# Small tables built ahead of the first loads, and a new order of the work, in a fused retention and token-mixing kernel

## The chip, the cores and the metric

The kernel runs on one core of one Trainium2 chip. A core has five engines with a queue of instructions each, taken in order: TensorE (PE, matrix products), VectorE (DVE), ScalarE (ACT), GpSimd (POOL) and SyncE (SP, which here only issues transfers). They meet through semaphores. The metric is the device time of one execution in microseconds (us).

## The reference, cut to what matters

Inputs are `q`, `k`, `v` of shape (4, 8, 768, 64) in fp32 (batch, heads, tokens, head size) and three weights. The first half is a linear attention with a decay per head:

```python
gamma = 1.0 - 2.0 ** (-5.0 - np.arange(H))
for t in range(S):
    state = gamma * state + einsum('bhd,bhe->bhde', k[:, :, t], v[:, :, t])
    y[:, :, t] = scale * einsum('bhd,bhde->bhe', q[:, :, t], state)
```

The heads of `y` are laid side by side as `x` (4, 768, 512), and the second half mixes tokens:

```python
wq = x @ w_q; wk = x @ w_k                       # 512 -> 64
W_tok = scale * einsum('bsd,btd->bst', wq, wk)   # tokens x tokens
mixed = einsum('bst,btd->bsd', W_tok, x)
out = maximum(mixed, 0) @ w_out
```

## The kernel before, in words

The 768 tokens of a batch are cut into three *pairs* of two chunks of 128 tokens; over four batches that makes pairs 0 to 11. Each pair goes through the same steps. Its `k`, `q` and `v` (512 KB each) are loaded into one of 27 slots of `stage` (`Lk`, `Lq`, `Lv`). They are cast to bf16 (`ck`, `cq`, on ACT, DVE or POOL) and, for `v`, scaled by a table of decay factors (`cv`, always on POOL). PE transposes `k` and `q` (`trk`, `trq`), and the results are copied out of PSUM (`ek`, `eq`). Scores are formed in two halves (`sc`) and masked to be causal while they leave PSUM (`eat`, DVE). The running state is accumulated on PE (`st`) and copied (`es`). The output of the attention sums the state's part (`in`) and the scores' part (`ia`) and is scaled by another table, `fy`, while it leaves PSUM (`ex`, DVE).

The second half of a pair: transpose `x` (`xt`, `exT`), its products with `w_q` and `w_k` (`wqk`, `ew`), a sum over the batch's three pairs (`zm`, `ez`), the mixed tokens (`mx`), their relu (`r`, ACT or DVE), the product with `w_out` in two chunks (`pj`, 512 columns), the copy out (`eo`) and the store (`S`). `W` and `WO` cast the weights. `zm` needs all three pairs of a batch, so the `mx` and `pj` of a batch come after the attention of its last pair.

PSUM has eight banks of 512 fp32 columns; bank 7 holds the state. The digits behind `@` in a step name the banks it uses, so a step also waits until the bank's former content has been copied out.

What sets the order is the string `ORDER` (lines 16 to 61), written out by a planner: one token per step, for instance `ck.3.0:A` (cast half 0 of `k` of pair 3 on ACT), `Lk.4=13` (load into slot 13) or `fill.4@2` (four products of zeros in bank 2, which only keep PE running). The loop at line 826 issues the steps in this order, so that each engine's queue has its share of the string in the string's order. An instruction that waits holds up all that stand behind it on its engine.

`KINDS` (line 63) has a letter for each pair, which says how its tokens lie over the partitions. In kind `2` a partition holds two neighbouring tokens, and both `k` and `v` are cast as they come, each half with one instruction of 128 partitions. Kind `R` has the same load, but `k` and `v` are brought into rows of chunks by two casts of 64 partitions for each half. Kind `M` is `R` for `k`, while `v` is loaded in four pieces of 128 KB (line 177) and cast by one instruction per half, with a table of its own, `fvM`.

The tables: `row` and `tok` (lines 235 to 247) hold each partition's token number; `fv` (line 250) and `fy` (line 255) are exponentials of 48 columns made on ACT at the start, after a product on DVE. The masks of kinds `2` and `R` are made on POOL by the steps `consts.2` and `consts.R` (lines 266 to 284: memset, select, and a copy for the lower 64 partitions). The table `fvM` is made by the step `constv.M` (lines 297 to 307), which stands in `ORDER` between steps of pair 5 and pair 7: two iotas, a copy and a product on POOL and then an exponential on ACT:

```python
        nc.gpsimd.tensor_tensor(out=t, in0=t, in1=ln_n, op=ALU.mult)
        nc.scalar.activation(out=f, in_=t, func=ACT.Exp)
```

`FIRST` (line 64) names the load that is issued ahead of all others in two halves, one from ACT's queue and one from SP's; before it is `q` of pair 0. All other transfers are issued by SP.

Of the kernel before, what the change touches and what calls it, by code (L numbers as in the profile page):

```python
# [16 lines left out]
fill.15@6 Lv.0=1 consts.2 cq.0.1:P cv.0.1:P Lk.0=2 cq.0.0:A Lq.1=3 ck.0.1:A ck.0.0:V Lk.1=4 Lv.1=5  # L17
Lk.2=6 Lq.3=7 consts.R cv.0.0:P Lq.2=8 Lk.3=9 Lv.2=10 cq.1.0:P cq.1.1:P Lv.3=11 ck.1.0:P LW=12
trq.0@0 cv.1.0:P cv.1.1:P Lk.4=13 trk.0@1 Lv.4=14 Lq.4=15 st.0.0 cq.2.1:P Lk.5=16 Lq.5=17 Lv.5=18
LO.1=19 ek.0:A LO.0=20 cq.3.0:P Lk.8=21 Lk.6=22 Lq.6=23 Lv.6=24 Lq.8=25 ck.3.1:P cv.2.0:P eq.0:V  # L20
cv.2.1:P Lk.7=26 es.0.0:V ck.1.1:A fill.1@2 sc.0.1@01 fill.4@2 trq.1@2 Lq.7=0 eat.0.1:V Lv.7=2
cv.3.0:P ck.2.0:A cv.3.1:P Lq.9=1 eq.1:V cv.4.0:P Lv.8=3 Lk.9=4 trk.1@01a Lv.9=5 Lk.10=10 ck.5.1:P
cv.4.1:P st.0.1 sc.0.0@23 ek.1:V es.0.1:V in.0.1@45 ck.2.1:A eat.0.0:V sc.1.0@01 Lq.10=6 eat.1.0:V
cq.2.0:A cq.3.1:A Lq.11=8 fill.3@6 ia.0.0@45 ia.0.1@45 st.1.0 sc.1.1@23 Lk.11=7 es.1.0:V eat.1.1:V
ex.0:V cv.5.0:P in.1.1@01 ia.1.0@01 WO.1:P Lv.10=11 in.1.0@01 ia.1.1@01 trk.2@2 fill.1@6 trq.2@3
ck.3.0:A fill.2@6 trq.3@45a st.1.1 ek.2:V eq.2:V eq.3:A ex.1:V es.1.1:V trk.3@45b sc.2.0@23 cv.5.1:P
eat.2.0:V xt.0@46a ek.3:A exT.0:A xt.1@0 W:A ck.4.0:A ck.4.1:A sc.2.1@15 eat.2.1:V in.2.0@23 st.2.0
fill.1@4 ia.2.0@23 Lv.11=9 es.2.0:V exT.1:V ia.2.1@23 in.2.1@23 st.3.0 sc.3.1@01 ex.2:V eat.3.1:V
sc.3.0@45 es.3.0:A wqk.0@6 xt.2@2 wqk.1@3 exT.2:V eat.3.0:V trk.4@0 ew.0:A cq.4.1:A cq.4.0:A st.3.1
fill.1@1 ia.3.1@26 wqk.2@1 ek.4:A trq.4@45a ck.6.0:P ck.8.1:P es.3.1:V ew.1:V cq.6.0:P in.3.1@26  # L30
ia.3.0@26 ck.5.0:A ck.6.1:P ew.2:V eq.4:V cv.6.0:P zm.0.0@3 zm.0.1@3 cv.6.1:P sc.4.1@45 sc.4.0@01
ez.0:A st.4.0 cq.5.1:A ex.3:V eat.4.1:V eat.4.0:V mx.2@23 es.4.0:A cq.5.0:A trk.5@6 constv.M
ck.7.1:P trq.5@45a xt.3@45b st.4.1 r.2.0:A r.2.1:A in.4.1@23 in.4.0@23 mx.0@01 exT.3:V cq.7.0:P
eq.5:A r.0.0:A ek.5:V ia.4.1@23 ia.4.0@23 wqk.3@4 r.0.1:A es.4.1:A sc.5.1@56 sc.5.0@01 cv.7.0:P
cv.7.1:P cv.8.1:P ex.4:V cv.8.0:P st.5.0 eat.5.0:V WO.0:A xt.4@2 pj.2.1@3 eat.5.1:V eo.2.1:A=12
pj.2.0@0 cv.9.0:P es.5.0:A ia.5.0@13 exT.4:V in.5.0@13 in.5.1@13 mx.1@56 r.1.0:V ia.5.1@13 ex.5:V
ew.3:V eo.2.0:A=12 pj.0.0@0 pj.0.1@2 ck.8.0:A xt.5@13a exT.5:V r.1.1:A eo.0.0:A=13 cq.6.1:A
trk.8@13b trk.6@04a trq.6@04b wqk.4@5 eq.6:A cq.8.0:A ek.8:V ek.6:V wqk.5@6 st.6.0 sc.6.0@04
cq.8.1:A ew.5:A ew.4:V sc.6.1@15 ck.10.1:P zm.1.0@3 ck.7.0:A eo.0.1:V=13 zm.1.1@3 cv.9.1:P eat.6.0:V
eat.6.1:V ez.1:A cq.7.1:A pj.1.1@6 cq.10.0:P cq.10.1:P cq.11.0:P cq.11.1:P trk.7@04a trq.8@04b  # L40
ck.11.0:P ck.11.1:P ek.7:V eo.1.1:A=15 mx.3@23 trq.7@15a pj.1.0@6 r.3.1:A r.3.0:A es.6.0:A eq.8:V
eq.7:V sc.8.1@04 cv.10.1:P cv.10.0:P mx.5@23 st.6.1 eo.1.0:A=15 r.5.1:A cq.9.1:A eat.8.1:V cq.9.0:A
r.5.0:A es.6.1:A ia.6.1@16 ia.6.0@16 in.6.1@16 ex.6:V sc.7.0@05 pj.3.1@4 st.7.0 sc.8.0@16 sc.7.1@23
eat.7.0:V eo.3.1:A=16 es.7.0:A pj.5.1@4 ck.9.0:A ck.9.1:A in.7.0@05 in.7.1@05 st.7.1 eat.7.1:V
ia.7.1@05 eat.8.0:V ia.7.0@05 trq.9@2 pj.3.0@3 ex.7:V xt.6@16a trk.9@16b eo.5.1:A=17 eq.9:A es.7.1:A
mx.4@05 r.4.0:A eo.3.0:V=16 st.8.0 r.4.1:A pj.5.0@2 ia.8.0@34 S.3 es.8.0:A ek.9:V exT.6:V
eo.5.0:A=17 sc.9.0@05 cv.11.0:P in.8.1@34 in.8.0@34 sc.9.1@16 st.9.0 S.5 es.9.0:A ck.10.0:A
eat.9.0:V ia.8.1@34 cv.11.1:P wqk.6@2 xt.7@0 pj.4.0@5 ew.6:A ex.8:V eat.9.1:V trk.10@2 st.9.1
trq.10@34a xt.8@34b in.9.1@16 eo.4.0:V=14 exT.7:A ek.10:A eq.10:V ia.9.0@16 ia.9.1@16 ex.9:V
pj.4.1@2 sc.10.1@05 exT.8:A eo.4.1:A=14 trq.11@34b sc.10.0@16 trk.11@34a wqk.8@2 eat.10.1:V ek.11:V  # L50
# [24 lines left out]
def kernel(  # L75
# [17 lines left out]

    nc = tc.nc
# [6 lines left out]
    U = 2  # L101
# [25 lines left out]
    def bank16(b):  # L127
        return banks[:, b].bitcast(BF16)
# [31 lines left out]
    def load(name, p, slot, part=None, eng=None):  # L160
# [7 lines left out]
        if KINDS[p] == "N" and name != "q":  # L168
# [60 lines left out]
    def iota(t, pattern, base, step, dtype=FP32):  # L229
# [5 lines left out]
    row = const_pool.tile([128, 3], mybir.dt.int32, name="row")  # L235
    tok = const_pool.tile([128, 1], FP32, name="tok")
# [5 lines left out]
    nc.vector.tensor_scalar(  # L242
        out=row[:, 1:2], in0=row[:, 0:1], scalar1=1, scalar2=U * (TG - 1), op0=ALU.logical_shift_left,
        op1=ALU.bitwise_and,
    )
    nc.vector.tensor_single_scalar(row[:, 2:3], row[:, 0:1], 6, op=ALU.logical_shift_right)
    nc.vector.tensor_tensor(out=tok, in0=row[:, 1:2], in1=row[:, 2:3], op=ALU.add)
# [635 lines left out]
```

## Time and profile before

| | |
|---|---|
| median of 3 runs | 153.59 us (152.68, 157.84, 153.59) |
| the profiled execution | 154.91 us, span of its instructions 153.2 us |
| mean granted TensorE clock in it | 0.833 |
| moved by DMA | 26.73 MB, of it 20.19 MB read from HBM |
| DMA busy share in 40 slices | near full until about 70 us, then low until the stores |

How to read the profile: times count from the span's start. "Busy" is the time in which an engine executed something. In a list of waits, `A <- B` means that an engine stood idle ahead of an instruction of line A until B released it. In a list in order of time each row has the start, the length, the engine, the line, the tiles (out<-in), the shape, the count, and in brackets the idle time ahead of it and what ended that. A busy PE is not a PE at its peak, since matmuls are pipelined. Rows of neighbouring instructions of one line are merged, under the first one's shape.

### The profile page before, as it was taken

The page shows a single profiled execution, that of the slowest core. Times are in us where ns is not written, and L with a number is a line of the kernel's source. Part 1 is how long each engine was busy: PE and PEld are TensorE (multiplying, and loading weights), DVE is VectorE, ACT ScalarE, POOL GpSimd, SP SyncE. Part 2 cuts the span into 40 slices and gives each one's busy share as a digit, 9 for nine tenths or more (in the row PEclk, how much of TensorE's full clock was granted, in tenths as well). Part 3 has the DMA queues.
Part 4 walks back from the last instruction along what each step waited for, and adds up shares of the span by engine and source line. Part 5 has one row for each costly group of instructions (what it writes and reads, how often), then busy time and mean ns, then how long its engine had stood idle before and what let it go on. Part 6 is the DMA issues. An engine that isn't in the chain of part 4 may idle for free.

```text
span 153.2 us, 3907 instructions
## 1 busy us (share of the span) xinstructions
PE 102.7 (67%) x1667; PEld 70.4 (46%) x1684; DVE 72.9 (48%) x117; ACT 65.4 (43%) x116; POOL 60.6 (40%) x89
## 2 busy tenths in 40 slices
PE   6958875599720997865365674569573766495990
PEld 2345554588520763743342443257452655263440
DVE  4045994567760376483533413143725733433460
ACT  4154256619404737537510705244244160435541
POOL 7599779879396699999100000000000000000000
PEclk9986999659985589999857655556999699999999
DMA  3999999999999999984000000342000000076394
GB/s 96 346 347 347 343 279 287 336 315 288 273 282 300 322 296 283 287 187 95 4 0 0 4 0 0 137 166 112 0 4 0 0 0 4 0 295 255 147 351 191
DMA packets 47169, 26.73 MB, mean 174 GB/s; under 512 B 8240, under 2 KB 44080, under 8 KB 47152
## 3 DMA queue, kind: packets, MB, share of 16 engines
q1 hardware_dynamic: 46624, 26.22, 56.1%
q10 hardware_dynamic: 528, 0.26, 0.6%
q8 instruction: 13, 0.21, 0.5%
q14 instruction: 4, 0.03, 0.1%
HBM read 20.19 MB, written 6.29 MB: 173 GB/s over the span
## 4 chain that ended last, share of the span: by engine, by line
PE 37%; SPq 21%; DVE 17%; ACT 9%; DMA 5%; issue 5%; POOL 4%; DVEq 0%; ACTq 0%; POOLq 0%
SPq L182 17%; PE banks L805 12%; DVE at L555 6%; DMA stage<-in_k_dram 5%; DVE x L685 5%; ACT relu L798 5%; PE banks L537 3%; SPq L199 3%; PE banks L664 3%; PE banks L727 2%; PE banks L738 2%; ACT qT L145 2%; PE banks L764 2%; DVE kT L146 2%; PE banks L694 2%
## 5 line engine op out<-in xcount | busy, mean ns | idle before, releaser
L805 PE MATMUL banks<-wout_sb,relu 128*128 128x512 bf16 x84 | 23.9, 406 | 9.5 <-DVE x L685 3.5
L555 DVE TENSOR_TENSOR at<-banks,maskR 128x1024 bf16<-128x1024 f32 x18 | 21.6, 1220 | 18.0 <-PE banks L537 7.6
L382 POOL TENSOR_TENSOR vs<-stage,fv 64x512 bf16<-64x512 f32 x24 | 25.0, 1043 | 2.9 <-DMA stage<-in_v_dram 1.5
L685 DVE TENSOR_TENSOR x<-banks,fy 128x1024 bf16<-128x1024 f32 x12 | 14.7, 1221 | 17.8 <-PE banks L664 7.7
L145 ACT COPY stage<-banks 128x512 f32<-128x512 f32 x15 | 8.7, 588 | 23.5 <-DVE at L555 6.9
L805 PEld LDWEIGHTS <-relu 128*128 128x128 bf16 x96 | 9.1, 103 | 18.4 <-issue 10.5
L145 ACT CAST ks<-stage 64x512 bf16<-64x512 f32 (+1 forms) x23 | 14.1, 616 | 6.6 <-DMA stage<-in_k_dram 6.3
L798 ACT ACTIVATE relu<-banks 128x512 bf16<-128x512 f32 x19 | 10.8, 597 | 11.8 <-PE banks L805 6.2
L146 POOL CAST ks<-stage 64x512 bf16<-64x512 f32 (+1 forms) x18 | 11.0, 609 | 5.7 <-DMA stage<-in_k_dram 5.0
L537 PE MATMUL banks<-qT,kT 64*128 64x128 bf16 x144 | 9.0, 263 | 5.7 <-DVE at L555 2.3
L328 PE MATMUL banks<-warm 128*128 128x512 bf16 x23 | 9.6, 575 | 1.8 <-DVE warm L218 1.3
L146 DVE COPY stage<-banks 128x512 f32<-128x512 f32 x9 | 6.1, 688 | 9.5 <-ACT relu L798 7.0
L537 PEld LDWEIGHTS <-kT 64*128 64x128 bf16 x144 | 6.0, 115 | 7.9 <-issue 6.6
L610 PE MATMUL banks<-s,qT 64*128 64x64 bf16 x128 | 4.2, 206 | 8.0 <-ACT relu L798 7.7
L664 PE MATMUL banks<-vs,at 128*128 128x64 bf16 x144 | 7.8, 209 | 2.6 <-DVE at L555 2.5
L727 PE MATMUL banks<-xT,wqk_w 128*128 128x256 bf16 x48 | 8.6, 309 | 1.4 <-DVE at L555 1.4
L145 ACT CAST qs<-stage 128x512 bf16<-128x512 f32 x13 | 7.7, 619 | 3.8 <-DMA stage<-in_q_dram 3.8
L555 DVE TENSOR_TENSOR at<-banks,mask 128x1024 bf16<-128x1024 f32 x6 | 7.2, 1222 | 3.6 <-ACT wqk_w L145 1.6
L571 PE MATMUL banks<-vs,ks 128*64 128x64 bf16 (+1 forms) x200 | 8.0, 217 | 1.3 <-POOL vs L363 0.9
L738 PE MATMUL banks<-wqk_w,xT 128*128 128x64 bf16 x96 | 8.7, 268 | 0.0
L664 PEld LDWEIGHTS <-at 128*128 128x128 bf16 x144 | 6.5, 108 | 4.5 <-issue 3.5
L146 DVE COPY kT<-banks 128x1024 bf16<-128x1024 bf16 x8 | 5.4, 685 | 5.9 <-PE banks L664 3.1
(89 smaller groups left out, 165.5 us busy)
## 6 DMA issues: line engine op xcount, KB each, us to landing
stage<-in_k_dram SPq DMA_DIRECT2D x12, 512.0 KB, 6.4
stage<-in_q_dram SPq DMA_DIRECT2D x11, 512.0 KB, 7.0
stage<-in_v_dram SPq DMA_DIRECT2D x9, 512.0 KB, 6.9
out_dram<-stage SPq DMA_DIRECT2D x9, 512.0 KB, 2.9
stage<-in_v_dram SPq DMA_DIRECT2D x12, 128.0 KB, 3.8
out_dram<-stage SPq DMA_DIRECT2D x6, 256.0 KB, 2.0
stage<-in_moe_w_out_dram SPq DMA_DIRECT2D x4, 256.0 KB, 4.5
stage<-in_q_dram ACTq DMA_DIRECT2D x1, 256.0 KB, 4.1
```

The source lines that it names most:

```text
L145: return nc.scalar.copy(out=out, in_=in_)
L146: return ENGINES[e].tensor_copy(out=out, in_=in_)
L182: eng.dma_start(out=st.rearrange("g (h f) -> g h f", h=H)[:, hs], in_=src.rearrange("h (g j) d -> g h (j d)", j=2)[:, hs],)
L382: eng.tensor_tensor(out=st["vs"][rows(j), c].rearrange("p hp x d -> p (hp x) d"), in0=src[rows(c), :, j], in1=fv[rows(c), cp, :, j].to_bro ...
L537: nc.tensor.matmul(out=at[:, x, hi, c], lhsT=kT[rows(x), hp, c], rhs=qT[rows(x), c, hp], start=(hi == 0 and c == 0), stop=(hi == 1 and c = ...
L555: ENGINES[e].tensor_tensor(out=st["at", half].rearrange("p x hi j t -> p x (hi j t)").rearrange("p x (n f) -> p x n f", n=n), in0=st["at_p ...
L664: nc.tensor.matmul(out=y[:, x, c, hp, :], lhsT=at[:, x, hi, c, :], rhs=vr[:, c, hp, x, :], start=first(p, x), stop=False, skip_group_check ...
L685: ENGINES[e].tensor_tensor(out=dst, in0=src, in1=f.to_broadcast([128, 2, H, D]), op=ALU.mult)
L727: nc.tensor.matmul(out=ps[:, 128:384], lhsT=wqk_sb[:, a, 0 : 2 * DH], rhs=st["xT"][:, a].rearrange("p c t -> p (c t)"), start=(a == 0), st ...
L738: nc.tensor.matmul(out=wk[:, c], lhsT=st["xT"][:, a, c, :], rhs=wqk_sb[:, a, 2 * DH :], start=False, stop=(a == NDM - 1), skip_group_check ...
L798: nc.scalar.activation(out=st["relu", c], in_=src, func=ACT.Relu)
L805: nc.tensor.matmul(out=bank32(b[0]), lhsT=st["relu", c][:, a // 2, a % 2, :], rhs=wout_sb[:, a, :], start=(a == 0), stop=(a == NDM - 1),)
```

## The change

It has three parts.

- **Tables and masks.** The tables of all kinds are made at the start: `decay` forms the product on DVE and the exponential on ACT, for `fy` and, behind it, for the table of kind `M` (`fvm`). The masks are made on DVE by comparing a row of token numbers, `tf` (an iota on POOL), with each partition's token number. The steps `consts` and `constv` are gone from `ORDER`, and no mask is made on POOL. The identity for the transposes stays on POOL and comes before the masks.
- **Kinds.** `KINDS` goes from `2R2RRR2RRMMM` to `2RR2R2RRRMRM`: pairs 0, 3 and 5 are of kind `2` (before 0, 2 and 6), and 9 and 11 of kind `M` (before 9, 10 and 11).
- **Order.** `FIRST` is `k` of pair 1. The whole `ORDER` is new, with the engine of each cast and copy: one `cv` is now on DVE, more casts of `k` are on ACT and fewer on POOL, both casts of `w_out` are on POOL, and the loads of `w_out` come behind those of pair 6.

`U` becomes a constant of the module with the value that it had; branches for `U == 8` are added and not taken. `trq` is rewritten with the same transposes.

The core of the diff; of `ORDER` only the stretches that the prediction speaks of:

```diff
-ez.0:A st.4.0 cq.5.1:A ex.3:V eat.4.1:V eat.4.0:V mx.2@23 es.4.0:A cq.5.0:A trk.5@6 constv.M
-ck.7.1:P trq.5@45a xt.3@45b st.4.1 r.2.0:A r.2.1:A in.4.1@23 in.4.0@23 mx.0@01 exT.3:V cq.7.0:P
...
+fill.15@6 Lq.0=1 cq.0.0:V ck.1.1:A cq.0.1:A Lk.0=2 Lv.0=3 trq.0@0 Lq.1=4 Lv.1=5 ck.1.0:P Lk.2=6
+Lq.3=7 Lq.2=8 Lv.2=9 eq.0:V ck.0.0:V cv.0.0:V fill.2@1 trk.1@12a Lk.3=10 LW=11 Lv.3=12 cv.0.1:P
+Lq.4=13 Lk.4=14 ck.0.1:A Lv.4=15 Lq.5=16 Lk.5=17 cv.1.0:P cq.3.1:P cv.1.1:P Lk.6=18 fill.6@3 trk.0@0
+cv.2.0:P Lv.5=19 Lv.6=20 Lq.6=21 LO.1=22 ck.3.1:P LO.0=23 Lk.7=24 Lk.8=25 cv.2.1:P ek.0:V Lq.7=26
...
+ck.5.1:A ck.7.0:P cv.6.1:P in.4.0@36 zm.0.1@0 xt.3@2 ez.0:A trk.5@5 st.4.1 eat.4.1:V in.4.1@36
+trq.5@1 cv.7.0:P cq.8.0:P ck.6.0:A cv.7.1:P ek.5:A ck.6.1:A ia.4.0@36 exT.3:V es.4.1:V eq.5:V
...
+pj.1.0@0 eat.6.0:V eo.1.1:V=11 es.6.0:V pj.2.0@4 ck.8.1:A ck.8.0:A eo.1.0:V=11 sc.6.1@26 mx.0@05
+cq.7.0:A eo.2.0:V=13 xt.5@13a trk.7@13b cq.7.1:A eat.6.1:V r.0.1:A ek.7:V r.0.0:V pj.2.1@4 st.6.1
...
-KINDS = "2R2RRR2RRMMM"
-FIRST = ('q', 0, 0)
+KINDS = "2RR2R2RRRMRM"
+FIRST = ('k', 1, 0)
...
+    def decay(name, tok, ln):
+        t = const_pool.tile([128, NP * 2, H], FP32, name="t" + name)
+        f = const_pool.tile([128, NP * 2, H], FP32, name=name)
+        nc.vector.scalar_tensor_tensor(out=t, in0=ty, scalar=tok, in1=ln, op0=ALU.add, op1=ALU.mult)
+        nc.scalar.activation(out=f, in_=t, func=ACT.Exp)
+        return f
+
+    fy = decay("fy", tok_q, ln_h)
+    fvs = {}
+    if "M" in KINDS:
+        fvs["M"] = decay("fvm", tok_r, ln_n)
...
+    def mask(name, toks):
+        t = const_pool.tile([128, len(toks), C], BF16, name=name)
+        for j, tok in enumerate(toks):
+            nc.vector.tensor_scalar(out=t[:, j], in0=tf, scalar1=tok, scalar2=None, op0=ALU.is_ge)
+        return t
...
-    def mask(name, nj, step, base2):
...
-            nc.gpsimd.memset(a, 1.0)
-            nc.gpsimd.affine_select(
...
-    def consts_v(kind):
...
-        nc.gpsimd.tensor_tensor(out=t, in0=t, in1=ln_n, op=ALU.mult)
-        nc.scalar.activation(out=f, in_=t, func=ACT.Exp)
-        fvs[kind] = f
```

More of the change, by code (lines that the diff above doesn't have):

```diff
@@ L22 @@
[L22 to L26, printed above, removed]
@@ L232, in iota @@
         )
-    row = const_pool.tile([128, 3], mybir.dt.int32, name="row")
-    tok = const_pool.tile([128, 1], FP32, name="tok")
+    row = const_pool.tile([128, 6], mybir.dt.int32, name="row")
     iota(row[:, 0:1], [[0, 1]], 0, 1)
@@ L390, in cq @@
         st = pairs[p]
+        if U == 8:
+            if "qs" not in st:
+                st["qs"] = new("qs", [128, U, 2, D])
+            copy(e, st["qs"][:, :, x], st["q_st"].rearrange("p (x u d) -> p x u d", x=2, u=U)[:, x])
+            return
         if "qs" not in st:
```

197 lines of the change are left out of this document (97 added, 100 removed).

## The prediction

> **What bounds the kernel now.** I read the page first, then the waits, then three engines' instructions in order of time around the longest wait, then busy time by stretch.
>
> ```profile
> PE 102.7 (67%) x1667; PEld 70.4 (46%) x1684; DVE 72.9 (48%) x117; ACT 65.4 (43%) x116; POOL 60.6 (40%) x89
> ...
> PE 37%; SPq 21%; DVE 17%; ACT 9%; DMA 5%; issue 5%; POOL 4%; DVEq 0%; ACTq 0%; POOLq 0%
> ```
>
> No engine is full, and the chain that ended last changes hands between PE, DVE and ACT. So the time lies in who waits for whom. The waits, longest first, have one pair that stands out:
>
> ```profile
> PE banks L610 <- ACT relu L798: 7.7, 2, 6.3
> ...
> ACT fvM L306 <- POOL tvM L305: 7.0, 1, 7.0
> ```
>
> ScalarE (ACT) stood still once for 7.0 us ahead of the exponential that `constv.M` issues, and TensorE (PE) once for 6.3 us. They are one event, as the three engines show in order of time (start, length, instruction):
>
> ```profile
> 40.60 0.62 ACT L145 CAST qs<-stage 128x512 bf16<-128x512 f32 x1
> 48.22 0.24 ACT L306 ACTIVATE fvM<-tvM 128x48 f32<-128x48 f32 x1 [7.00 <-POOL tvM L305]
> 48.37 1.06 ACT L798 ACTIVATE relu<-banks 128x512 bf16<-128x512 f32 x2
> ```
> ```profile
> 34.23 2.14 POOL L382 TENSOR_TENSOR vs<-stage,fv 64x512 bf16<-64x512 f32 x2 [0.74 <-DMA stage<-in_v_dram]
> ...
> 42.03 1.96 POOL L146 CAST ks<-stage 128x512 bf16<-128x512 f32 x3 [2.33 <-DMA stage<-in_k_dram]
> ...
> 47.91 0.28 POOL L305 TENSOR_TENSOR tvM<-tvM,ln_n 128x48 f32<-128x48 f32 x1
> 49.29 1.28 POOL L146 CAST ks<-stage 64x512 bf16<-64x512 f32 x2 [1.10 <-DMA stage<-in_k_dram]
> ```
> ```profile
> 36.87 0.60 PE L727 MATMUL banks<-xT,wqk_w 128*128 128x256 bf16 x4
> 37.31 0.61 PE L738 MATMUL banks<-wqk_w,xT 128*128 128x64 bf16 x8
> ...
> 39.42 0.62 PE L537 MATMUL banks<-qT,kT 64*128 64x128 bf16 x16
> ...
> 41.22 0.40 PE L783 MATMUL banks<-m,z 64*128 64x256 bf16 x4 [0.93 <-ACT qs L145]
> ...
> 42.92 0.32 PE L571 MATMUL banks<-vs,ks 128*64 128x64 bf16 x8
> 49.49 0.61 PE L610 MATMUL banks<-s,qT 64*128 64x64 bf16 x16 [6.26 <-ACT relu L798]
> ...
> 51.30 1.04 PE L727 MATMUL banks<-xT,wqk_w 128*128 128x256 bf16 x4
> 52.14 1.06 PE L738 MATMUL banks<-wqk_w,xT 128*128 128x64 bf16 x8
> 53.13 1.04 PE L537 MATMUL banks<-qT,kT 64*128 64x128 bf16 x16
> ```
>
> To be read from the bottom up: PE at 49.49 (`in.4`) waits for a bank that ACT's relu of pair 2 must empty. That relu's input was there at 41.62 (41.22 + 0.40), but on ACT it stands behind the exponential, which needs the table that GpSimd (POOL) multiplies at 47.91. POOL was late because `ck.6`, ahead of it, waited for its load until 42.03. A table of 48 columns thus tied PE to a load of another pair. Busy time by stretch:
>
> ```profile
> core 0: us, PE busy (x) PEld busy (x) DVE busy (x) ACT busy (x) POOL busy (x), PEclk, DMA share, GB/s
> 0.00:11.00 11.00, 8.17 (x48) 3.62 (x48) 3.17 (x36) 3.91 (x7) 7.85 (x24) 0.98 0.87 259
> 11.00:41.20 30.20, 23.82 (x524) 18.73 (x529) 21.34 (x28) 16.65 (x28) 24.77 (x28) 0.84 1.07 314
> 41.20:49.50 8.30, 1.84 (x54) 1.48 (x54) 3.42 (x4) 1.30 (x5) 6.04 (x12) 0.71 0.94 275
> ...
> 70.00:128.40 58.40, 36.31 (x602) 26.48 (x608) 23.50 (x24) 22.64 (x42) 3.49 (x4) 0.74 0.09 31
> 128.40:153.20 24.80, 15.43 (x131) 8.02 (x132) 9.64 (x13) 9.42 (x17) 0.00 (x0) 1.00 0.50 191
> ```
> ```profile
> 49.50:54.50 5.00, 5.00 (x73) 3.87 (x73) 1.46 (x2) 3.13 (x5) 3.75 (x6) 0.50 1.09 324
> ```
>
> POOL leads until 41.2 (24.77 of 30.2 us), and is all but done by 70. From 70 on only PE, DVE (VectorE) and ACT work, each with gaps, for 83.2 us of 153.2.
>
> **The change, part by part.** I sum against the profiled execution: 154.91 us, span 153.2, so 1.7 lie around the span. The median of the three times is 153.59, which is 1.3 lower; at the end I take that off.
>
> *1. The table `fvM`.* Its product and exponential move to the start, behind `fy`. The ACT wait of 7.0 goes; what the path has of it is PE's 6.26. What is late next? Without the wait the two relus (1.06) start at about 41.65 and end at 42.7, before PE has finished at 43.24 (42.92 + 0.32); `in.4.1` can then follow at once. So 6.3 goes in full: **-6.3**. Were something else late there, it would be zero.
>
> *2. The slow matmuls behind the gap.* The granted clock was 0.50 from 49.5 to 54.5, and groups that took 0.60, 0.61 and 0.62 before the gap took 1.04, 1.06 and 1.04 after it. With no gap these three give back 0.44 + 0.45 + 0.42 = 1.3. The most would be 5.00 us of PE at 0.50 made at 1.00, thus 2.5; the least is nothing, if the new order has a gap of its own. DVE and ACT have work between the groups, so I take the three: **-1.3**. [...]
>
> *3. The masks.* POOL loses two memsets, two selects and a copy for each of two masks. The first set ended before its first cast; the second lies between two `cv` steps:
>
> ```profile
> 7.82 0.29 POOL L273 TENSOR_SCALAR_AFFINE_SELECT maskR<-maskR 128x128 bf16<-128x128 bf16 x1
> 8.06 0.20 POOL L272 MEMSET maskR_b<- 128x128 bf16 x1
> 8.33 0.35 POOL L273 TENSOR_SCALAR_AFFINE_SELECT maskR_b<-maskR_b 128x128 bf16<-128x128 bf16 x1
> 8.75 0.29 POOL L283 COPY maskR<-maskR_b 64x128 bf16<-64x128 bf16 x1
> 9.12 1.05 POOL L363 TENSOR_TENSOR vs<-stage,fv 128x512 bf16<-128x512 f32 x1
> ```
> ```profile
> 8.00 0.55 DVE L146 CAST ks<-stage 128x512 bf16<-128x512 f32 x1 [4.67 <-DMA stage<-in_k_dram]
> ```
>
> That frees up to 1.5 us of POOL at 7.6 to 9.1. In the new order `cv.0.1` has no such work ahead, but v of pair 0 is now the fourth half-megabyte and not the second; one covers the other, so 0 (bounds -1.5 and 0). DVE gets three compares of 128 columns and a few one-column operations. The trace has no such compare; below the cast of 512 columns (0.55), above nothing: I take 0.2 each, 1 us with the small ones, all inside the 4.67 us in which DVE waited for its first load. If that cover were gone it would cost that 1 us. ACT's third small exponential (0.24 by the row at 48.22) stands ahead of `ck.1.1` and lies in its wait for the first load.
>
> *4. `cv.0.0` on DVE* (0.6 us by the cast's row, at most the 1.05 of POOL's) beside POOL's `cv.0.1`: both wait for v of pair 0, and behind `cv.0.0` on DVE stands `ek.0`, for which PE's first scores wait. It ends before POOL's, which the first state step needs too: 0. [...] The nearest row, the select at 8.33 beside DVE's cast, took 0.35 where its twin took 0.29; no row here has the pair itself. [...]
>
> *5. Casts change hands.* By the two orders ACT has 26 half-tile k casts instead of 20, one more whole one, three more q casts, two more of xT and three more of kT; it loses two of qT, a weight cast, a z, a relu and one output copy, and has one more of s.
>
> ```profile
> L382 POOL TENSOR_TENSOR vs<-stage,fv 64x512 bf16<-64x512 f32 x24 | 25.0, 1043 | 2.9 <-DMA stage<-in_v_dram 1.5
> ...
> L145 ACT CAST ks<-stage 64x512 bf16<-64x512 f32 x20 | 12.3, 616 | 2.3 <-DMA stage<-in_k_dram 2.0
> ```
>
> At 0.6 a cast and 1.0 a transposed tile ACT gains about 7 us; POOL loses as much, DVE gains 1. Up to the step `st.4.1` (42.92 above), ACT had about 20 us of such work; in the new order about 26 (10 half-tile and 4 whole k casts 8.6, 9 of q 5.6, 8 tiles of kT, qT and xT 8.1, weights 1.1, 5 of s and one z 2.3). It has to fit between 11 and 41.2 us, where ACT was busy 16.65 of 30.2: nothing is lost if the six go into the gaps, 6.0 if none does. DVE lived with 21.34 in the same stretch; with six more ACT has 22.7. That is the nearest row, so I stay near the lower end: **+1.5**.
>
> *6. Loads.* Bytes are the same, and so each half-megabyte lands when its place in the queue did. k of pair 6 moves from place 22.5 to 18.5, where v of pair 5 came at 34.23: 7.8 us earlier than 42.03. k of pair 7 goes from 26.5 (49.29) to 24.5, k of 8 to 25.5, q of 7 to 26.5: about 45.6, 47.5, 49.3. With k of pair 1 in front, q of pair 0 comes one place later, some 1.5 us; but k of pair 0, which the first scores need, stays third (8.00 in the rows of part 3). SP issues the later loads with fewer waits, since the slots are free long before. One pair fewer has its v in four pieces, for which POOL pays two casts of 1.043 more (in POOL's count above). Nothing on the path: 0.
>
> *7. The new order after 56 us.* The same matmuls but for nine more warm-up fills, early, in front of waits for loads; the order from the last `ia.11` on has twelve `pj` steps in both, seven of them after the last `mx`, so the last 24.8 us stay. Between, no PE wait is longer than this one:
>
> ```profile
> PE banks L537 <- DVE at L555: 2.3, 1, 2.3
> ```
>
> so one such more or less: 0, bounds -2.3 and +2.3.
>
> Sum: 154.91 - 6.3 - 1.3 + 1.5 = 148.8, and with the 1.3 to the median **147.5 us**.
>
> **The rivals.**
> *A. ACT bounds the front.* All six us of part 5 land on the path: 4.5 more, 152.0. For it: ACT takes its work in order, and its casts wait for loads. Against it: 13.5 us of ACT's stretch are idle.
> *B. Slower: PE at half rate.* If ACT, filled with casts, hands out banks in bursts, PE gets gaps like the one at 43 again, and the clock stays at 0.50 where it was 0.74 (70 to 128.4). PE has 37% of the chain: 21.6 of these 58.4 us become 32.0, 10.4 more: 157.9. It decides from a mean below about 0.60 on. For it: 0.74 shows how near it is. Against it: the longest wait there is 2.3.
> *C. More gain.* The six us vanish into gaps, the slow matmuls give back 2.5 and one wait of 2.3 goes: 147.5 - 1.5 - 1.2 - 2.3 = 142.5. Beyond that the loads stop it: `cq.7.0`, ahead of a relu on ACT, can't run before 49.3.
> *D. The table isn't what held PE.* If another of pair 4's inputs came at 49 as well, parts 1 and 2 are nothing: 153.59 + 1.5 = 155.1. Its conditions (bank, state, qT) were all met by 43 in the rows above, which speaks against it.
>
> **How the numbers follow.** The forecast, 145 to 150.5: 0.50. C: 0.13. A: 0.15, D: 0.06, both within 2%, which is about what a measurement of this kernel can tell from no change (150.5 to 156.7). B: 0.16. So faster 0.63, same 0.21, slower 0.16. Eight in ten: from 142 (C) to 155.5 (past A and D); B and a bit more stay out.
>
> **What would show it.** After: the exponentials all before 4 us; no ACT wait for POOL of several us; PE without a gap over 3 us between 35 and 55, clock 0.7 or more there (parts 1, 2); `st.4.1` at 41 to 45 (part 5); ACT near 72 us, POOL near 53; the end 24 to 26 us after the last `ia.11`. Wrong would be: a new long wait of PE for ACT behind a k or q cast, or a clock below 0.6 in the long middle.

## The result, and the profile after

The changed kernel takes **165.67 us** (median of four runs, 165.25 to 170.26); the kernel before took 154.25 us beside it. The ratio is **1.077 [1.067, 1.087]**: slower, where the forecast was 147.5 and faster. Some executions of each of these kernels run a few per cent longer at a lower granted clock: the ratios, here and further down, leave them out (a cell is empty where there is no ratio), the medians don't, and the profiled execution, 170.26 us with a span of 168.5 at a clock of 0.737 (0.75 to 0.77 in the others), is one of them, so what follows goes by where time stands in it and not by differences of a few us.

Busy time of the changed kernel by engine, from the page:

```profile
PE 117.9 (70%) x1694; PEld 78.1 (46%) x1709; DVE 74.5 (44%) x124; ACT 73.0 (43%) x126; POOL 53.3 (32%) x67
```

ACT and POOL are where the forecast had them (72 and 53). TensorE is busy 15 us longer with nearly the same instructions: its mean granted clock was 0.74, for 0.83 before. By stretch of time (busy us of each engine, granted clock, DMA share, GB/s):

```profile
core 0: us, PE busy (x) PEld busy (x) DVE busy (x) ACT busy (x) POOL busy (x), PEclk, DMA share, GB/s
0.00:11.00 11.00, 9.56 (x61) 4.17 (x64) 5.46 (x44) 4.46 (x9) 4.21 (x13) 1.00 0.88 263
11.00:41.20 30.20, 18.78 (x368) 13.79 (x370) 14.44 (x15) 16.59 (x27) 21.64 (x23) 0.69 1.08 318
41.20:49.50 8.30, 6.83 (x127) 5.70 (x121) 2.11 (x3) 1.08 (x2) 6.00 (x8) 0.50 1.12 330
49.50:56.50 7.00, 4.46 (x44) 3.24 (x44) 2.86 (x4) 3.25 (x6) 5.70 (x7) 0.50 1.05 293
...
143.00:168.50 25.50, 17.72 (x128) 8.53 (x128) 8.55 (x12) 7.98 (x14) 0.00 (x0) 0.89 0.32 124
```

The stretch 11 to 41.2 is the one to compare with the same row of before. There PE made 524 matmuls and VectorE (DVE) 28 instructions; here it is 368 and 15. PE, DVE and POOL work less, and ACT no more than before (16.59 for 16.65), where the forecast put 22.7 into the same time. Nothing became the bound; the engines wait more. How far this runs, by the scaling of pair 3 (`ex.3`) of before, and then the same step and the step `st.4.1` of after:

```profile
39.94 1.23 DVE L685 TENSOR_TENSOR x<-banks,fy 128x1024 bf16<-128x1024 f32 x1 [0.82 <-ACT z L145]
```
```profile
53.66 1.23 DVE L704 TENSOR_TENSOR x<-banks,fy 128x1024 bf16<-128x1024 f32 x1 [2.49 <-PE banks L556]
...
60.02 0.42 PE L590 MATMUL banks<-vs,ks 128*64 128x64 bf16 x8
```

`ex.3` is 13.7 us late, and `st.4.1`, at 42.92 before and forecast for 41 to 45, is 17.1 late. The whole loss (11.4 us by the medians) is there before 60 us.

Who waits for whom? The groups of the mask product and of the scaling in the changed kernel, with the idle time ahead of them and its three largest releasers:

```profile
L574 DVE TENSOR_TENSOR at<-banks,maskR 128x1024 bf16<-128x1024 f32 x18 | 21.8, 1220 | 23.7 <-PE banks L824 5.6 <-ACT stage L145 5.0 <-PE banks L683 4.0
L704 DVE TENSOR_TENSOR x<-banks,fy 128x1024 bf16<-128x1024 f32 x12 | 14.6, 1220 | 16.1 <-PE banks L824 5.8 <-PE banks L683 4.2 <-PE banks L556 4.1
```

This is the odd part. The scaling (L704) reads the attention's output, which L629 and L683 make. Line 824 is the product with `w_out`, line 556 the scores of another pair: neither makes anything that the scaling reads. One case in order of time, the scaling of pair 1 (`ex.1`, banks 1 and 5), first PE, then DVE:

```profile
24.77 0.27 PE L629 MATMUL banks<-s,qT 64*128 64x64 bf16 x7 [1.18 <-DVE x L704]
26.13 0.61 PE L517 MATMUL banks<-identity,qs 64*128 64x64 bf16 x16 [1.09 <-ACT kT L145]
...
29.51 0.61 PE L556 MATMUL banks<-qT,kT 64*128 64x128 bf16 x8 [0.36 <-issue]
```
```profile
27.82 0.69 DVE L146 COPY qT<-banks 128x1024 bf16<-128x1024 bf16 x1 [3.11 <-ACT qT L145]
30.16 1.22 DVE L704 TENSOR_TENSOR x<-banks,fy 128x1024 bf16<-128x1024 f32 x1 [1.65 <-PE banks L556]
```

Its input was complete at 25.04 (24.77 + 0.27). It started at 30.16, when the scores `sc.2.1@03` had ended (29.51 + 0.61 = 30.12). Those go to banks 0 and 3, and bank 3 lies between 1 and 5. The copy ahead of it on DVE, `eq.3` out of bank 2, had waited 3.11 us for ACT's `eq.2` out of banks 0 and 3, and bank 2 lies between those. From this came the theory of the **ranges**: an instruction that takes two banks in one strided access waits for what other engines do in any bank from the lower to the upper, not in its own two alone. The digits in `ORDER` allow a count. Of the 102 steps of before that name two banks, 56 name neighbours, and among the first 60 steps with banks 32 of 37 do. In the new order it is 31 of 104, and at the start 4 of 35 (`@03`, `@15` and `@46` are the usual ones). The rivals against it: casts that fill ACT (rival A of the prediction), and the clock as a cause of its own (rival B).

The trace and `ORDER` together also allow a count of the waits themselves. In the kernel before, 22 waits of ACT or DVE of over 0.15 us ahead of a copy or product out of PSUM (49.4 us in all) ended with such an instruction on the other engine. In 16 of them (38.4 us) the two share no bank, but their ranges meet; in five (8.6 us) they share one; one (2.4 us) fits neither. In the changed kernel it is 15 of 20 (42.7 of 50.5 us), two and three, and the last three (6.7 us) aren't explained by ranges.

### The profile page after: what moved, and what is told of

Same layout as the page of the kernel before. It is cut to its first block, busy times and chain, and to the rows that moved or that the text cites. A ratio compares the mean times of both kernels' runs of the same rounds, so it can differ in the third digit from the quotient of the medians.

```text
span 168.5 us, 3951 instructions
## 1 busy us (share of the span) xinstructions
PE 117.9 (70%) x1694; PEld 78.1 (46%) x1709; DVE 74.5 (44%) x124; ACT 73.0 (43%) x126; POOL 53.3 (32%) x67
## 5 line engine op out<-in xcount | busy, mean ns | idle before, releaser
L824 PE MATMUL banks<-wout_sb,relu 128*128 128x512 bf16 x85 | 28.8, 467 | 9.6 <-ACT relu L817 3.8
L574 DVE TENSOR_TENSOR at<-banks,maskR 128x1024 bf16<-128x1024 f32 x18 | 21.8, 1220 | 23.7 <-PE banks L824 5.6
L399 POOL TENSOR_TENSOR vs<-stage,fv 64x512 bf16<-64x512 f32 x28 | 29.2, 1043 | 8.3 <-DMA stage<-in_v_dram 6.9
L704 DVE TENSOR_TENSOR x<-banks,fy 128x1024 bf16<-128x1024 f32 x12 | 14.6, 1220 | 16.1 <-PE banks L824 5.8
L145 ACT CAST ks<-stage 64x512 bf16<-64x512 f32 (+1 forms) x30 | 18.5, 617 | 3.0 <-DMA stage<-in_k_dram 2.7
L145 ACT COPY xT<-banks 128x1024 bf16<-128x1024 bf16 x7 | 7.1, 1015 | 17.1 <-PE banks L802 7.7
L145 ACT COPY kT<-banks 128x1024 bf16<-128x1024 bf16 x7 | 7.0, 1012 | 14.3 <-DVE at L574 5.7
L345 PE MATMUL banks<-warm 128*128 128x512 bf16 x33 | 11.5, 486 | 2.4 <-DVE warm L224 1.2
L746 PE MATMUL banks<-xT,wqk_w 128*128 128x256 bf16 x48 | 11.0, 375 | 2.6 <-DVE xT L146 1.8
L146 DVE COPY qT<-banks 128x1024 bf16<-128x1024 bf16 x9 | 6.1, 688 | 12.1 <-PE banks L629 4.4
L757 PE MATMUL banks<-wqk_w,xT 128*128 128x64 bf16 x96 | 10.6, 304 | 0.0
L145 ACT CAST s<-banks 128x256 bf16<-128x256 f32 x15 | 5.6, 374 | 10.0 <-PE banks L590 10.0
L757 PEld LDWEIGHTS <-xT 128*128 128x128 bf16 x96 | 9.4, 154 | 1.1
L683 PE MATMUL banks<-vs,at 128*128 128x64 bf16 x144 | 7.5, 212 | 3.3 <-ACT relu L817 3.3
```

Source lines behind the costliest of these rows:

```text
L145: return nc.scalar.copy(out=out, in_=in_)
L146: return ENGINES[e].tensor_copy(out=out, in_=in_)
L345: nc.tensor.matmul(out=bank32(b), lhsT=warm[:, 0:128], rhs=warm, start=True, stop=True)
L399: eng.tensor_tensor(out=st["vs"][rows(j), c].rearrange("p hp x d -> p (hp x) d"), in0=src[rows(c), :, j], in1=fv[rows(c), cp, :, j].to_bro ...
L574: ENGINES[e].tensor_tensor(out=st["at", half].rearrange("p x hi j t -> p x (hi j t)").rearrange("p x (n f) -> p x n f", n=n), in0=st["at_p ...
L683: nc.tensor.matmul(out=y[:, x, c, hp, :], lhsT=at[:, x, hi, c, :], rhs=vr[:, c, hp, x, :], start=first(p, x), stop=False, skip_group_check ...
```

## The experiments

All times are medians. The kernel before ran beside each group on the same chip and took 154.3 to 156.2 there. "Tables alone", "renamed", "spread" and "split" are told below, each where its runs come.

| kernel | us | against before |
|---|---|---|
| changed kernel | 165.67 | 1.077 [1.067, 1.087] |
| tables alone | 148.06 | |
| changed, banks renamed | 130.23 | |
| before, banks renamed | 133.16 | 0.856 [0.843, 0.870] |
| before, banks spread | 184.45 | |
| tables alone, banks renamed | 122.61 | 0.799 [0.795, 0.804] |
| changed, renamed up to `st.4.1` | 144.38 | 0.939 [0.929, 0.948] |
| changed, renamed from `st.4.1` on | 147.82 | 0.956 [0.941, 0.971] |
| changed, six casts to POOL | 181.46 | 1.174 [1.155, 1.193] |
| changed, split | 106.36 | 0.686 [0.673, 0.700] |
| changed, renamed and split | 104.64 | 0.679 [0.671, 0.687] |
| before, spread and split | 114.23 | 0.741 [0.732, 0.750] |
| before, split | 113.94 | 0.742 [0.734, 0.751] |
| tables alone, split | 101.55 | 0.654 [0.643, 0.666] |
| tables alone, renamed and split | **101.06** | 0.654 [0.640, 0.668] |
| changed, split, `cv.0.0` on POOL | 103.63 | 0.674 [0.663, 0.685] |
| changed, only DVE's products split | 127.41 | 0.823 [0.808, 0.838] |

### The tables alone

The changed kernel with `KINDS`, `FIRST` and the string `ORDER` of before; only the steps `consts.2`, `consts.R` and `constv.M` are taken out of the string.

```diff
-KINDS = "2RR2R2RRRMRM"
-FIRST = ('k', 1, 0)
+KINDS = "2R2RRR2RRMMM"
+FIRST = ('q', 0, 0)
```

> The new tables and masks with the order, kinds and first load of before. If the wait of ACT for the table fvM held PE for 6.3 us, as the prediction's parts 1 and 2 have it, this runs 6.3 to 7.6 us faster than before: 146.5 to 148. If something else of pair 4 or 5 came as late (rival D), it stays within 2 us of before. If making the tables on VectorE at the start costs, it is slower.

148.06 (146.13 to 150.35) beside 154.75: 6.7 faster, and 6.9 by the two quickest executions (146.13 and 146.42) against the three quickest of before (152.21 to 153.71). So parts 1 to 3 of the prediction, 7.6 together, hold. Everything else in the change (parts 4 to 7, forecast at +1.5) makes the 148.06 into 165.67, 17.6 us longer; what loses lies in the new order.

### Renaming the banks

The digits of `ORDER` go through a list before they are used; nothing else changes, neither the order of the steps nor the engines, nor which steps share a bank. (The two digits of a step are sorted after it, so the halves of a pair can swap banks.) In the changed kernel 62 of the 104 pairs then are neighbours (31 before), in the kernel before 71 of 102, and in the spread one 4 of 102.

```diff
+BANK = (1, 2, 5, 0, 6, 3, 4)
...
-            b = ["ab".index(i) if i in "ab" else int(i) for i in b]
+            b = sorted(BANK[int(i)] for i in b if i not in "ab") + ["ab".index(i) for i in b if i in "ab"]
```

For the kernel before the list is `(2, 1, 6, 5, 4, 3, 0)`, and spread `(3, 1, 2, 5, 0, 6, 4)`.

> The changed kernel, with nothing but the seven PSUM banks of the order renamed among themselves (0 to 6 become 1,2,5,0,6,3,4), so that the pairs of banks used together lie side by side more often. Theory (spans): a step that touches two banks b0 and b1 also waits for steps on the banks between them, and the new order has such pairs far apart in its first third; then this is at least 6 us faster than the changed kernel, 160 or less. Rival (casts): ACT, filled with casts, bounds the front; the names of banks change nothing, 165 to 166. Rival (clock): the granted clock is low because PE draws more; again 165 to 166.

> Before, with nothing but its banks renamed (0 to 6 become 2,1,6,5,4,3,0), which brings pairs closer in its last two thirds. Spans: faster by 2 to 6 us, 148 to 152, with the 7 us wait for the table still there. Casts or clock: within 1 us of before.

> Before, with its banks renamed so that pairs lie far apart (0 to 6 become 3,1,2,5,0,6,4). Spans: slower by 8 us or more, 162 or more, with VectorE and ScalarE waiting in the first third as they do in the changed kernel. Casts or clock: within 1 us of before, since no engine gets other work.

The order of before takes 133.2, 154.8 and 184.5 us with 71, 56 and 4 neighbouring pairs; the new order takes 130.2 and 165.7 with 62 and 31. The names alone move each kernel by more than any part of the change was forecast to. With good names the changed kernel is no slower than the one before, though ACT does the same work as in the changed kernel with its own names, by the page of the renamed one:

```profile
PE 94.9 (74%) x1694; PEld 62.6 (49%) x1709; DVE 73.5 (58%) x124; ACT 72.6 (57%) x126; POOL 53.2 (42%) x67
```

So rival A doesn't explain the slowdown. What the fuller ACT costs beside it isn't shown here: the tables alone, with renamed banks, are still faster than this kernel (next run). PE's 94.9 us, for 117.9 with the same matmuls, show the clock: its mean in the profiled executions is 0.93 here and 0.74 in the changed kernel, 0.90 and 0.73 in the kernel before with good and with spread names. Only the names differ within each of the two, so the clock follows the waits and isn't a cause of its own.

### The tables with renamed banks

The two edits above together: the tables alone, with the list `(2, 1, 6, 5, 4, 3, 0)`.

```diff
+BANK = (2, 1, 6, 5, 4, 3, 0)
```

> The order of before, with the tables of after (as in the run with the tables alone, 148.1) and with the banks of before renamed 2, 1, 6, 5, 4, 3, 0 (as in the run that took before from 154.8 to 133.2). If the table of pair 9 to 11 and the ranges of banks are two independent losses, the 6.7 of the tables comes off the 133.2: about 126.5. If the wait for the table was partly a wait for banks, 130 to 133.

122.61 (122.49 to 122.99), 10.6 below the renamed kernel before (8.9 by the two ratios). Independent losses would have given 6.7; that the late table costs more once other waits are gone is shown further down. The renamed changed kernel, with the new order besides, took 130.23 (its quickest execution 125.53). So with good names too the new order gains nothing; it costs 7.6 by the medians and 3.0 by the quickest executions.

### Where the ranges cost

The list is used only ahead of `st.4.1`, as in the diff, or (with `False`) only from there on. At the border some banks are written under their new name before they have been read under the old one, so these two compute something else from there; the instructions are the same.

```diff
+LAST = ORDER.index("st.4.1")
...
+            m = BANK if (n < LAST) == True else range(7)
```

> The changed kernel with the banks renamed 1, 2, 5, 0, 6, 3, 4 only in the steps ahead of st.4.1 (which came at 60.0 in after, at 42.9 in before). Ranges of banks, acting where they stand: the first 60 us lose about 17 us, the rest keeps its length, so 147 to 150. If a delay of the front is all there is, and the rest followed from it: 130, as with all steps renamed. If the names of the banks worked in another way than by the ranges in the steps that use them: 165.

> The changed kernel with the banks renamed only in the steps from st.4.1 on. Ranges of banks, acting where they stand: st.4.1 stays at 60 and the rest gives what the other run doesn't, so 146 to 150 (the two gains add up to the 35 of the whole renaming). If a delay of the front is all there is: 165.

144.38 and 147.82: 21.3 and 17.9 below the changed kernel, 39.2 together, where the whole renaming gave 35.4 by the medians and 39.7 by the quickest execution of each. So the ranges act where they stand, in both halves. The front, which lost 17, gives back somewhat more than it lost.

### Casts from ACT to POOL

```diff
-sc.0.0@45 fill.1@6 sc.1.1@12 sc.1.0@03 es.0.1:V eat.0.0:V eat.1.1:V eat.1.0:V ck.2.1:A fill.2@6
-ia.0.1@46 in.0.1@46 cv.5.0:P cv.5.1:P in.1.0@15 st.1.0 ia.0.0@46 cq.3.0:A ck.2.0:A Lk.10=7 Lk.11=6
-trq.3@2 Lq.10=12 fill.2@0 trk.2@03a ia.1.1@15 ia.1.0@15 cq.2.1:A es.1.0:A cq.2.0:A ex.0:V in.1.1@15
+sc.0.0@45 fill.1@6 sc.1.1@12 sc.1.0@03 es.0.1:V eat.0.0:V eat.1.1:V eat.1.0:V ck.2.1:P fill.2@6
+ia.0.1@46 in.0.1@46 cv.5.0:P cv.5.1:P in.1.0@15 st.1.0 ia.0.0@46 cq.3.0:P ck.2.0:P Lk.10=7 Lk.11=6
+trq.3@2 Lq.10=12 fill.2@0 trk.2@03a ia.1.1@15 ia.1.0@15 cq.2.1:P es.1.0:A cq.2.0:P ex.0:V in.1.1@15
...
-ex.2:V sc.3.0@26 wqk.1@5 st.3.0 WO.0:P cq.4.1:A cq.4.0:A trq.4@0 es.3.0:V ck.4.0:A ck.4.1:A
+ex.2:V sc.3.0@26 wqk.1@5 st.3.0 WO.0:P cq.4.1:A cq.4.0:A trq.4@0 es.3.0:V ck.4.0:P ck.4.1:A
```

> The changed kernel with six casts ahead of st.4.1 (both of k of pair 2, both of q of pair 2, one of q of pair 3, one of k of pair 4) on POOL instead of ACT, some 5 us of work, banks as they are. Casts on ACT as the cause (rival A): up to 5 us faster, 160 to 163. Ranges of banks: ACT's own work isn't what its queue waits for, so 165.7 within 2 us, ACT's busy time near 68 and POOL's near 58.

181.46, 16 us slower than the changed kernel; neither theory had that. The waits of this kernel, and then POOL in order of time:

```profile
PE banks L513 <- POOL qs L146: 18.0, 1, 18.0
```
```profile
36.07 2.05 POOL L380 TENSOR_TENSOR vs<-stage,fv 128x512 bf16<-128x512 f32 x2 [0.38 <-DMA stage<-in_v_dram]
38.06 0.61 POOL L146 CAST qs<-stage 128x512 bf16<-128x512 f32 x1
```

`cq.3.0` now stands on POOL behind both `cv` of pair 5, which waited for their load until 36.07; PE waited 18.0 us for it. ACT's queue was the better place for this cast. Since the move made a trap of its own, the run says nothing for or against rival A, though ACT had less work (67.3 us).

### Two instructions of one bank each

The direct test of the ranges: the names stay, and each copy out of two banks is made bank by bank. This holds for the mask product, the scaling, the relu, and those transposed tiles that lie in two banks.

```diff
+    def by_bank(do, out, in_, in1=None, **kw):
+        for i in range(2):
+            more = {} if in1 is None else dict(in1=in1[:, i : i + 1])
+            do(**{"out": out[:, i : i + 1], "in_" if in1 is None else "in0": in_[:, i : i + 1]}, **more, **kw)
...
-        ENGINES[e].tensor_tensor(out=dst, in0=src, in1=f.to_broadcast([128, 2, H, D]), op=ALU.mult)
+        by_bank(ENGINES[e].tensor_tensor, dst, src, f.to_broadcast([128, 2, H, D]), op=ALU.mult)
...
-            nc.scalar.activation(out=st["relu", c], in_=src, func=ACT.Relu)
+            by_bank(nc.scalar.activation, st["relu", c], src, func=ACT.Relu)
```

> The changed kernel with its own names of the banks; every copy out of two banks is made as two instructions of one bank each (the mask product, the scaling, the relu and the transposed tiles that lie in two banks: some 75 instructions more, on DVE and ACT). If an instruction on two banks waits for all banks between them: no instruction has a range any more, so most of the 35 us of the renaming is won without it; the extra instructions cost some 0.1 to 0.2 each, 8 to 15 us of DVE and ACT together, half of it on the path: 135 to 145. If what the names change is something of the banks themselves (which of them are used one after another): 165.7 plus the extra instructions, 168 to 178.

> The order of before with the banks renamed 3, 1, 2, 5, 0, 6, 4, which made it 184.5, and with every copy out of two banks made as two instructions. Ranges: the names no longer matter, so it comes near what before takes with good names, 133, plus the extra instructions: 133 to 145. Something of the banks themselves: 184 or more.

> The kernel of 122.6 (tables of after, order of before, banks renamed 2, 1, 6, 5, 4, 3, 0) with every copy out of two banks made as two instructions. If few ranges are left there, only the extra instructions show: 123 to 130. If ranges still cost several us: below 122.

> The changed kernel with the banks renamed 1, 2, 5, 0, 6, 3, 4 (130.2) and every copy out of two banks made as two instructions. By the ranges it and the split kernel with its own names have no range left, so both take the same time within 3%, and the rest of what the new order costs or gains shows against the order of before treated in the same way: 122 to 135.

106.36, 114.23, 101.06 and 104.64. The first, second and fourth lie below every one of their ranges; the third is the "below 122" of ranges that still cost, by far more than the several us expected. The split changed kernel, by its page and its groups:

```profile
PE 90.1 (86%) x1694; PEld 60.2 (57%) x1709; DVE 76.8 (73%) x178; ACT 73.5 (70%) x156; POOL 53.3 (51%) x67
```
```profile
L151 DVE TENSOR_TENSOR at<-banks,maskR 128x512 bf16<-128x512 f32 x36 | 22.6, 684 | 3.4 <-PE banks L564 2.7 <-ACT s L145 0.5 <-issue 0.2
L151 DVE TENSOR_TENSOR x<-banks,fy 128x512 bf16<-128x512 f32 x24 | 15.3, 684 | 1.4 <-PE banks L678 1.1
```

The idle time ahead of the mask product falls from 23.7 to 3.4 us and ahead of the scaling from 16.1 to 1.4, and the foreign releasers are all but gone: line 564 makes the scores, line 678 the scores' part of the output, and only 0.5 us on ACT's copy of the state is left. My two errors of size: I took the 35 us of the renaming for all there was, though 42 of the 104 pairs were still apart; and I priced the extra instructions at 8 to 15 us, where two halves of a product cost 2 x 0.684 for 1.220, and DVE's busy time grew by 2.3 us and ACT's by 0.5.

Once split, the names no longer count. Spread names, which cost the order of before 30 us, take 114.23 against 113.94 with its own (below); renamed or not, the changed kernel takes 104.64 and 106.36 with overlapping intervals, and the tables alone 101.06 and 101.55. That is what the theory asks for: without strided accesses to two banks there is no range for a name to change.

How much of the gain is ranges alone isn't settled. A half also empties its bank and hands on its output sooner than the whole instruction does (0.684 us for 1.220), with any names, and no run prices that. Of the 59.3 us that the split takes off the changed kernel, the names alone account for 35.4; the other 23.9 are the ranges of the 42 pairs that were still apart, the sooner halves, or both.

### What the change is worth without ranges

The same split for the kernel before, for the tables alone, and for the changed kernel with one cast back on POOL; and in a fourth kernel, with only the mask products and the scaling split.

```diff
-Lq.3=7 Lq.2=8 Lv.2=9 eq.0:V ck.0.0:V cv.0.0:V fill.2@1 trk.1@12a Lk.3=10 LW=11 Lv.3=12 cv.0.1:P
+Lq.3=7 Lq.2=8 Lv.2=9 eq.0:V ck.0.0:V cv.0.0:P fill.2@1 trk.1@12a Lk.3=10 LW=11 Lv.3=12 cv.0.1:P
```

> The kernel before, with its own names of the banks and its late table, and every copy out of two banks made as two instructions. By the ranges the names no longer count: 114 like the run with spread names, within 3% (111 to 118). The wait for the table of pair 9 to 11 is still in it. Against the changed kernel treated the same way (106.4) it shows what the change is worth where no ranges stand in the way; the forecast's sum of parts 1 to 7, 6.1 faster, would put this one at 112.5.

> The tables and masks of the change with the order and the names of before, and every copy out of two banks made as two instructions. By the ranges the names don't count, so 101.1 as with the renamed banks, within 3% (98 to 104). The difference to the split kernel before is parts 1 to 3 alone (forecast 7.6 faster together); the difference to the split changed kernel (106.4) is parts 4 to 7, which would then be 5 slower, where the forecast had 1.5.

> The split changed kernel (106.4) with the first cv of pair 0 on POOL instead of DVE (part 4 undone). If the product on DVE holds POOL's up (1.46 for 1.04 in after): POOL's two products take 1.04 each, the second ends some 0.6 later than now, and the time stays within 1 us of 106.4. If part 4 is worth something on the path: more than 1 us slower, or faster.

> The changed kernel with only the mask products and the scaling made as two instructions of one bank each (36 more, nearly all on DVE); relu and transposed tiles still leave two banks at once where they lie in two. Ranges of DVE's products the main part: near 106 to 120. Ranges of ACT's relu and copies as large: 130 to 150. If the split instructions won because DVE's work got shorter pieces and not because of ranges: as fast as the whole split, 106.

Before 113.94, tables alone 101.55, whole change 106.36. So with split copies the change makes the kernel **7.6 faster**, where the sum of the prediction's parts was 6.1 at the same point. The tables are worth 12.4 there; the waits of the split kernel before say why:

```profile
ACT fvM L314 <- POOL tvM L313: 12.7, 1, 12.7
PE banks L619 <- ACT relu L151: 12.6, 1, 12.6
```

POOL in order of time:

```profile
43.46 1.95 POOL L146 CAST ks<-stage 128x512 bf16<-128x512 f32 x3 [2.83 <-DMA stage<-in_k_dram]
...
49.34 0.28 POOL L313 TENSOR_TENSOR tvM<-tvM,ln_n 128x48 f32<-128x48 f32 x1
```

The table still stands behind casts of k that wait for their load, while the other engines come there sooner: ACT waits 12.7 us for it instead of 7.0. Everything else in the change (parts 4 to 7) then costs 4.8, where the forecast had 1.5.

With `cv.0.0` back on POOL the time is 103.63, where up to 1 us of difference was expected if only POOL's product was held up. Three of its four executions (102.83 to 104.27) are quicker than any with the product on DVE (105.03 to 106.94), but the intervals (0.663 to 0.685 and 0.673 to 0.700) overlap, so a gain of up to 2.7 isn't settled, and the rest of the 4.8 stays open.

Splitting the mask products and the scaling alone takes the changed kernel to 127.41: 38 of the 59 us; the other 21 come only with the relu and the transposed tiles. The shorter pieces of these products aren't all that wins, since they are the same in both; whether they are a part of the 38 this run doesn't tell.

The tables with the split copies, at 101.06 and 101.55, are the fastest: a third less than the kernel before. PE is busy 90% of the span in the latter:

```profile
PE 91.0 (90%) x1684; PEld 60.9 (61%) x1684; DVE 76.7 (76%) x178; ACT 66.6 (66%) x143; POOL 57.2 (57%) x76
```

## Why the prediction was wrong

The account, by medians: splitting takes 165.7 - 106.4 = 59.3 off the changed kernel and 154.4 - 113.9 = 40.5 off the kernel before. So what the split removes cost the new kernel 18.8 more than the old one, against the 7.6 that the change gains where it is gone. (That these two make up the measured loss of 11.4, but for the 0.2 between two groups of runs, follows from the subtraction and is no further evidence; the evidence is the renamed and the split kernels.)

**Part 7 is the step that failed.** It put the new order at nothing, with one wait of 2.3 as a bound, because the matmuls are the same. It priced instructions and compared the steps' places, and took the digits behind `@` for names. What the runs showed in its place: parts 4 to 7 cost 17.6 us (165.67 against 148.06 with the tables alone), forecast at +1.5, and 35.4 us of the changed kernel hang on the digits alone. My text before it even had the rule that a step waits until its bank has been emptied, but I didn't ask which banks an instruction waits for. Its other half is nearly right: the last `ia.11` ends at 142.16 (the group of PE at 141.15, 1.01 long), and the end comes 26.3 us later (forecast 24 to 26), in the longest of the executions.

The profile of before showed it, and I read past it. Two of its groups, for which the prediction had no use:

```profile
L145 ACT COPY stage<-banks 128x512 f32<-128x512 f32 x15 | 8.7, 588 | 23.5 <-DVE at L555 6.9 <-PE banks L805 6.7 <-DVE x L685 5.5
L146 DVE COPY stage<-banks 128x512 f32<-128x512 f32 x9 | 6.1, 688 | 9.5 <-ACT relu L798 7.0 <-PE banks L805 2.4
```

The copy of the final output (`eo`) reads one bank that L805 fills. It can have nothing to wait for but L805 and a free slot; it waited 12.4 us (6.9 + 5.5) for mask products and scalings, and 7.0 for a relu. In order of time on ACT, the two waits of 12.4 us:

```profile
84.03 0.58 ACT L145 COPY stage<-banks 128x512 f32<-128x512 f32 x1 [6.92 <-DVE at L555]
...
92.78 0.58 ACT L145 COPY stage<-banks 128x512 f32<-128x512 f32 x1 [5.46 <-DVE x L685]
```

By their place in `ORDER` these are `eo.3.1` and `eo.5.1`, both out of bank 4 (`pj.3.1@4`, `pj.5.1@4`), and what they waited for are the mask product and the scaling of pair 7, both out of banks 0 and 5. The same two groups in the split kernel before:

```profile
L145 ACT COPY stage<-banks 128x512 f32<-128x512 f32 x15 | 8.9, 594 | 7.0 <-PE banks L814 6.8
L146 DVE COPY stage<-banks 128x512 f32<-128x512 f32 x9 | 6.2, 688 | 4.2 <-ACT m L145 2.2 <-PE banks L814 1.7 <-ACT relu L151 0.3
```

On ACT what is left is the wait for L814, which makes the output there. On DVE one wait of 2.2 us for ACT's copy `m` out of another bank remains, and ranges don't explain it.

**Parts 1 and 2** were right where they stand alone: the exponentials now run at the start, and no wait of ACT for POOL is left.

```profile
2.52 0.24 ACT L278 ACTIVATE fv<-tv 128x48 f32<-128x48 f32 x1
2.67 0.23 ACT L285 ACTIVATE fy<-tfy 128x48 f32<-128x48 f32 x1
2.81 0.23 ACT L285 ACTIVATE fvm<-tfvm 128x48 f32<-128x48 f32 x1
```

Alone with part 3 they gave 6.7 of the forecast 7.6, and with the tables alone the granted clock was 1.00 from 41.2 to 60, where the kernel before had 0.71 up to 49.5 and then 0.50 up to 54.5. In the changed kernel too PE had no gap over 3 us between 35 and 55 (the longest, which ended at 40.68, is 2.5), but the clock of 0.7 didn't come: it was granted 0.50 from 41.2 to 56.5, so part 2 gave nothing there. In the kernel before, the 0.50 came behind 6.26 us of idle time, and part 2 took the one for the effect of the other. Here no wait of PE from 11 us on had been over 2.52: from 41.2 to 56.5 it worked 11.3 of 15.3 us and waited at most 1.83 at a time, and had the halved clock all the same. What had halved it isn't shown.

**Part 3** was right: the compares take 0.24 to 0.28 each (I took 0.2) and are over at 3.3, while DVE's first cast waits for its load until 6.24.

```profile
2.65 0.48 DVE L309 TENSOR_SCALAR mask<-tf,tok 128x128 bf16<-128x128 f32 x2
3.04 0.28 DVE L309 TENSOR_SCALAR maskR<-tf,tok_r 128x128 bf16<-128x128 f32 x1
...
6.24 0.43 DVE L146 CAST qs<-stage 128x512 bf16<-128x512 f32 x1 [2.68 <-DMA stage<-in_q_dram]
```

**Part 4** is unsettled. DVE's product takes 0.69, and POOL's beside it 1.46 in the split changed kernel; with both on POOL, two take 2.05. First the former, then the latter:

```profile
9.60 1.46 POOL L388 TENSOR_TENSOR vs<-stage,fv 128x512 bf16<-128x512 f32 x1 [3.40 <-DMA stage<-in_v_dram]
```
```profile
9.54 2.05 POOL L388 TENSOR_TENSOR vs<-stage,fv 128x512 bf16<-128x512 f32 x2 [3.40 <-DMA stage<-in_v_dram]
```

So POOL loses 0.43 beside DVE. DVE's product runs from 9.45 to 10.14 there and POOL's from 9.60, so the two lie beside each other for 0.54 us, a little more than was lost; why POOL's takes longer isn't shown.

**Part 5** had the work right (ACT 73.0, forecast near 72). The time isn't shown by itself: parts 4 to 7 together cost 4.8 without ranges. That ACT can hold the six us shows in the split changed kernel, by stretch of time:

```profile
11.00:41.20 30.20, 26.86 (x700) 21.20 (x702) 26.42 (x48) 27.05 (x52) 20.83 (x23) 1.00 1.05 304
```

ACT is busy 27.05 of 30.2 us there, and PE makes 700 matmuls in a stretch that had 368. But `st.4.1`, forecast for 41 to 45, came at 60.02 in the changed kernel. **Part 6** held: `ck.7.0` starts at 43.66 behind a wait for its load, 1.9 us sooner than the landing was forecast (45.6).

**The rivals.** B had the symptom (clock 0.50 to 0.76 between 11 and 128) and the sign, but the wrong place and cause: it wanted ACT's casts to hand out banks in bursts after 70, and the loss was there at 60. The kernel came out slower, as B had it, but for another reason, so B was right by luck. D falls with the tables alone. A, at most 6.0 us of loss on the path, can't make the 17.6; whether it is in the 4.8 that parts 4 to 7 cost with split copies stays open. None of them had ranges.

## What to carry to other kernels

In a list of waits, ask of each pair whether the one's output is the other's input, or lies where the other writes; where it is neither, the wait may be one that the program's bookkeeping added, and an edit that moves no work can show it, as new names did here. (Releasers in a profile are inferred, so a single odd pair proves nothing.) In this program a strided access to two PSUM banks was ordered against the banks between as well (new names took 35.4 us off the changed kernel, two instructions in its place 59.3): make it two instructions, or at least name the banks so that pairs are neighbours. What puts that order into the program, the runs don't show. And a new order of the same work is not a term of zero: what it names counts as well as what it does.

## What the runs showed that I had not expected

- Renaming banks, with no other edit, moved the order of before between 133.2 and 184.5 us, and splitting its two-bank copies took 26% off its time (0.742 [0.734, 0.751]).
- A reader of one bank also waited for another engine's reader of two banks around it: the output copies above waited 6.92 us for a mask product and 5.46 for a scaling, and none of them writes a bank.
- In the changed kernel the granted clock was 0.50 for 15 us in which no wait of PE was over 1.83 us; the mean clock was 1.00 over the 99.0 us span of the fastest kernel.
- The same product of 128x1024 on DVE takes 1.220 us whole and 2 x 0.684 in halves: a split costs 0.15.
